# A hand-ordered prologue on one Trainium2 core: four loads, four value projections and two half units in another order

## The chip, the cores and the metric

The kernel runs on one NeuronCore of a Trainium2 chip. The metric is the device time of one execution in microseconds (us), and the time before is the median of three runs: 222.35 us (222.42, 222.35 and 222.23).

## The reference, cut to what matters

There are 2048 tokens of width 512, and `x` is used by both branches. `D` is 512, `F` is 1792.

```python
xn = layernorm(x)                                # no scale, no shift, eps 1e-5
q, k, v = split(xn @ wqkv)                       # 32 heads of 16
phi(t) = concat(softmax(t @ w_phi), softmax(-t @ w_phi))
kv = sum_s phi(k)[s]^T v[s] ;  z = sum_s phi(k)[s]
o = (phi(q) @ kv) / (phi(q) @ z + 1e-6)
out = x + o @ wo + ((xn @ w_gate) * (xn @ w_up)) @ w_down
```

## The kernel before, in words

The tokens are 16 tiles of 128 (`NT`), in four groups of four. Everything TensorE needs of a tile is its normalized and transposed form `xnT`, four chunks of 128 features by 128 tokens. Once that exists, a tile feeds three kinds of work:

- **v projection** (`vproj`, before.py's line 332, matmuls on L252): four matmuls 128x512 that accumulate in one PSUM bank, which is then copied to `vt` (L339).
- **a unit** (`unit`, L281): for one block of 128 hidden features and a whole group of tokens, four matmuls of the gate weights `wg` (name `g`), four of the up weights `wu` (name `u`), both on L288. ScalarE copies the gate to SBUF (`g_sb`, L294), VectorE multiplies (`hT`, L297). A half unit does two of the four tiles, with matmuls 128x256.
- k and q features, the attention and the output (`fin`), all later.

For the first group the normalization is done by hand, tile by tile: VectorE's statistics (L161, then an aggregate on L367, L382 or L393), ScalarE's square root (`std`, L371), VectorE's reciprocal (L375) and the application (`xn`, L177). TensorE transposes the four chunks into one PSUM bank (`tp`, L219), and ScalarE copies them to `xnT` in two halves (L223). The later groups take another path (`ln_block` and transposing DMAs), and the change doesn't touch it.

The order of the work is written out by hand: a manual schedule holds TensorE, VectorE, ScalarE, GpSimd and the SyncE queue to the order of the program text. All loads are issued by SyncE in that order too, on one queue (L74 to L100): x tiles 0 and 1, `wv` in two halves, x tiles 2 and 3, the first two blocks of `wg` and then of `wu`, `wphi`, and so on.

[...]

Before the first tile is ready, nine matmuls of constants (`warm_up(9)`, L324) keep TensorE at work; a tenth stands behind tile 0's transposes. Then TensorE's order is: transposes of tile 0, the warm-up, the first half of v of tile 0, transposes of tile 1, the rest of v of tile 0, v of tile 1, gate of half unit 0, transposes of tile 2, its up, gate of half unit 1, transposes of tile 3, its up, v of tiles 2 and 3. Then come the second halves of the two units (`for f in range(2)`, tiles 2 and 3), full units, the fold of the k weights (L243), and so on to the end without a further wait of note.

Of the kernel before, what the change touches and what calls it, by code (L numbers as in the profile page):

```python
# [8 lines left out]
BF16 = mybir.dt.bfloat16  # L9
F32 = mybir.dt.float32  # L10
# [11 lines left out]
def kernel(  # L22
# [51 lines left out]
    def dma_x(lo, hi):  # L74
        nc.sync.dma_start(out=xall[:, lo:hi, :], in_=x_view(lo, hi))  # L75
# [4 lines left out]
    def dma_gu(lo, hi):  # L80
        dma_cols(nc.sync, wg, B_w_gate, lo * P, hi * P)
        dma_cols(nc.sync, wu, B_w_up, lo * P, hi * P)
# [3 lines left out]
    for lo in (0, 2):  # L86
        nc.sync.dma_start(out=wv[:, lo:lo + 2, :],  # L87
                          in_=A_wqkv[lo * P:(lo + 2) * P, 2 * D:3 * D].rearrange("(c p) f -> p c f", p=P))
    dma_x(2, 3)
    dma_x(3, 4)  # L90
    dma_gu(0, 2)
    nc.sync.dma_start(out=wphi[:], in_=A_w_phi.rearrange("(c h) d f -> (h d) c f", c=DC))
    dma_gu(2, 4)
    nc.sync.dma_start(out=wT2[:, 1, :, :], in_=A_wqkv[:, D:2 * D], transpose=True)
# [12 lines left out]
    def table(func, i):  # L107
        nc.scalar.activation(out=first[:, i:i + 1], in_=ones[:, 0:1], func=func, scale=1.0)
# [45 lines left out]
    def bank(name, dt=F32, n=TT):  # L154
        return ps_s.tile([P, n], dt, name=name, tag="s")
# [3 lines left out]
    def ln_sums(n):  # L159
        stats = lnpool.tile([P, nc.vector.BN_STATS_DIM], F32, name="stats")  # L160
        nc.vector.bn_stats(out=stats[:], in_=xall[:, n, :])  # L161
        return stats
# [18 lines left out]
    def mv_tile():  # L181
        return lnpool.tile([P, GT, nc.vector.BN_AGGR_DIM], F32, name="mv", bufs=GT)
# [30 lines left out]
        for i in range(GT):  # L213
            chores.append(lambda i=i: apply(i))

    def lt(n, parts=1, later=False):
        tp = bank("tp", BF16).rearrange("p (c t) -> p c t", c=DC)
        for c in range(DC):
            nc.tensor.transpose(out=tp[:, c, :], in_=xns[n][:, c * P:(c + 1) * P], identity=ident[:])  # L219

        def copies():
            for c in range(0, DC, DC // parts):
                nc.scalar.copy(out=xnT[:, c:c + DC // parts, n * P:(n + 1) * P], in_=tp[:, c:c + DC // parts, :])  # L223

        if later:
            return copies
        copies()

    bd = consts.tile([P, DC, 8, DH], BF16)

# [19 lines left out]
    def proj(ps, n, w, js=range(DC)):  # L250
        for j in js:
            nc.tensor.matmul(ps, lhsT=xnT[:, j, n * P:(n + 1) * P], rhs=w[:, j, :],  # L252
                             start=(j == 0), stop=(j == DC - 1))
# [24 lines left out]
    hTs = {}  # L278
    units = [(T, f) for T in range(NGRP) for f in range(FC)]

    def unit(T, f, lo=0, hi=TT, amid=None):  # L281
        if T not in hTs:
            hTs[T] = hpool.tile([P, FC, TT], BF16, name="hT", tag="h")
        pss = []
        for w, name in ((wg, "g"), (wu, "u")):
            ps = bank(name)[:, 0:hi - lo]
            for c in range(DC):
                nc.tensor.matmul(ps, lhsT=w[:, c, f * P:(f + 1) * P], rhs=xnT[:, c, T * TT + lo:T * TT + hi],  # L288
                                 start=(c == 0), stop=(c == DC - 1))
            pss.append(ps)  # L290
            if amid is not None and name == "g":
                copies = amid()
        g_sb = gpool.tile([P, TT], BF16, name="g_sb")
        nc.scalar.copy(out=g_sb[:, 0:hi - lo], in_=pss[0])  # L294
        if amid is not None:
            copies()
        nc.vector.tensor_tensor(out=hTs[T][:, f, lo:hi], in0=pss[1], in1=g_sb[:, 0:hi - lo], op=ALU.mult)  # L297

    def ffn(k):
        for _ in range(k):  # L300
# [18 lines left out]

    warm = bank("warm")  # L320

    def warm_up(k):
        for _ in range(k):
            nc.tensor.matmul(warm, lhsT=ones[:, 0:P], rhs=ones, start=True, stop=True)  # L324

    warm_up(9)

    with tc.tile_pool(name="ps_k", bufs=1, space=PSUM) as ps_k:
        kvps = [ps_k.tile([P, 4, 4, E1], F32, name=f"kv{b}") for b in range(2)]
        phiks = {}  # L330

        def vproj(n, copy=nc.scalar.copy, amid=None, later=False):
            ps = bank("pv")
            proj(ps, n, wv, range(2))
            if amid is not None:
                amid()
            proj(ps, n, wv, range(2, DC))
            def evict():
                copy(out=vts[n % NV][:, :, :, 0:DH], in_=ps.rearrange("p (a b c) -> p a b c", a=8, b=4))  # L339
            if later:  # L340
                return evict
            evict()

        def kproj(n, pf=None):
            phiks[n] = features(n, W1k, "k", pf)

        def vkproj(n):
            pv, pk = bank("pv"), bank("k")
            for j in range(DC):
                proj(pv, n, wv, (j,))  # L350
                proj(pk, n, W1k, (j,))
            nc.scalar.copy(out=vts[n % NV][:, :, :, 0:DH], in_=pv.rearrange("p (a b c) -> p a b c", a=8, b=4))  # L352
            kproj(n, pk)

        def kv(n):
            vt, phik = vts[n % NV], phiks[n]
            for gr in range(NG):
                nc.tensor.matmul(kvps[gr // 4][:, gr % 4, :, :].rearrange("p a b -> p (a b)"),  # L358
                                 lhsT=phik[:, gr, :], rhs=vt[:, gr, :, :].rearrange("p a b -> p (a b)"),
                                 start=(n == 0 and gr % 4 == 0), stop=(n == NT - 1 and gr % 4 == 3))  # L360

        mvs = [mv_tile() for n in range(GT)]
        stds = {}

        def first_stats(n):
            stats = ln_sums(n)
            nc.vector.bn_aggr(out=mvs[n][:, 0, :], in_=stats[:])  # L367

        def first_std(n):
            stds[n] = lnpool.tile([P, 1], F32, name="std", bufs=GT)  # L370
            nc.scalar.activation(out=stds[n][:], in_=mvs[n][:, 0, 1:2], func=AF.Sqrt, bias=epst[:], scale=1.0)  # L371

        def first_apply(n):
            rstd = lnpool.tile([P, 1], F32, name="rs1", bufs=GT)
            nc.vector.reciprocal(out=rstd[:], in_=stds[n][:])  # L375
            ln_apply(n, mvs[n][:, 0, 0:1], rstd[:])

        first_stats(0)
        first_std(0)
        stats1 = ln_sums(1)  # L380
        first_apply(0)
        nc.vector.bn_aggr(out=mvs[1][:, 0, :], in_=stats1[:])  # L382
        first_std(1)
        first_apply(1)
        first_stats(2)
        stats3 = ln_sums(3)
        lt(0, parts=2)
        warm_up(1)
        copy_v = vproj(0, amid=lambda: lt(1, parts=2), later=True)
        first_std(2)  # L390
        first_apply(2)
        copy_v()
        nc.vector.bn_aggr(out=mvs[3][:, 0, :], in_=stats3[:])  # L393
        first_std(3)
        first_apply(3)
        make_bd()
        nc.gpsimd.tensor_tensor(out=M4[:], in0=BO[:, 0:4, :], in1=BO[:, 4:8, :], op=ALU.add)
        vproj(1)
        unit(0, 0, 0, 2 * P, amid=lambda: lt(2, parts=2, later=True))
        unit(0, 1, 0, 2 * P, amid=lambda: lt(3, parts=2, later=True))  # L400
        vproj(2, copy=nc.vector.tensor_copy)
        vproj(3, copy=nc.vector.tensor_copy)
        table(AF.Exp, 1)
        for f in range(2):
            unit(0, f, 2 * P, TT)
        del units[0:2]
        ffn(1)
        for j0 in (0, 2):
            fold(1, W1k, j0, (nc.scalar.copy, nc.vector.tensor_copy))
        ffn(1)  # L410
        ln_block(4)
        ffn(1)
        chore(2)
        kproj(0)
        ffn(1)
        chore(2)
        ffn(1)
        chore()
        kproj(1)
        ffn(1)  # L420
        chore()
        ffn(1)
        kproj(2)
        chore()
        ffn(1)
        kv(0)
        chore()
        ffn(1)
        kproj(3)
        chore()  # L430
        ffn(1)
        kv(1)
        nc.sync.dma_start(out=wT2[:, 0, :, :], in_=A_wqkv[:, 0:D], transpose=True)
        for n in range(GT, NT):
            if n in (4, 8):
                ln_block(n + 4)
            vkproj(n)
            chore(1 if n % GT < 2 else 0)
            ffn(1)
            kv(n - 2)  # L440
            chore((1, 2, 2, 2)[n % GT])
            if n >= 8 and n % 2 == 0:
                qproj((n - 8) // 2)
            if n == 6:
                fold(0, W1q, 0)
            ffn(1)
            if n == 6:
                fold(0, W1q, 2)
        ffn(1)
        kv(NT - 2)  # L450
        ffn(1)
        kv(NT - 1)
        for b in range(2):
            nc.vector.tensor_tensor(out=KV[:, 4 * b:4 * b + 4, :, :], in0=kvps[b][:],
                                    in1=_bcast_ap(M4[:], [M4[:].ap[0], [0, 4], [E1, 4], [1, E1]]), op=ALU.mult)
        qproj(4)
        ffn(1)
# [64 lines left out]
```

## Time and profile before

| what | value |
|---|---|
| median of three runs | 222.35 us |
| the profiled execution's own time | 222.45 us |
| its span, first to last instruction | 220.7 us |
| TensorE (PE) busy | 215.6 us, 98% of the span |
| VectorE (DVE), ScalarE (ACT), GpSimd (POOL) busy | 138.7, 89.5, 68.8 us |
| last transposes of the first group (tile 3) start | 10.25 us |
| second halves of the two units start on TensorE | 12.64 us |
| first fold starts | 16.21 us |

Times are counted from the start of the span. A line of the timeline has the start, the length, the engine, the line of the program, the operation, what it writes and reads, and how many instructions were merged; in brackets stands how long the engine had been idle, and what released it. PEld is the loading of a stationary operand, which can run beside a matmul. Matmul lengths in the profile reach past the start of the next one, so TensorE's pace is read from starts, not from lengths.

### The profile page before, as it was taken

The numbers are of one execution on the slowest core, as the hardware profiler recorded it, in microseconds if no ns is written. First come the engines' busy times: TensorE is split into PE (matmuls) and PEld (weight loads), VectorE is DVE, ScalarE is ACT, GpSimd is POOL, SyncE is SP. The second block draws the span as 40 slices with busy tenths as digits, with TensorE's granted clock in tenths as the row PEclk, the third lists the DMA queues.
The fourth block names the chain that finished last, engine by engine and source line by source line (L and its number), as shares of the span: only waits on it lengthen the run. The fifth ranks groups of instructions, "written<-read, shape, count | busy, mean of one in ns | idle before, by whom it ended". The sixth has DMA issues, their size and how long they took to land.

```text
span 220.7 us, 3490 instructions
## 1 busy us (share of the span) xinstructions
PE 215.6 (98%) x1284; PEld 104.8 (47%) x1308; DVE 138.7 (63%) x241; ACT 89.5 (41%) x170; POOL 68.8 (31%) x54
## 2 busy tenths in 40 slices
PE   8999999999999999999999999999999999999994
PEld 2554444445444444444544444444444444454443
DVE  4657985785569685757589964197645745454321
ACT  3755575449764875545353221231322323100000
POOL 3000455545335653637333643033033033000000
PEclk9999999999999999999999999999999999999999
DMA  5999983503200324020206645214431431422401
GB/s 182 237 310 386 367 217 69 97 0 48 31 18 12 57 43 81 9 42 1 49 1 96 119 97 109 62 24 95 95 74 24 95 71 28 91 52 71 71 27 48
DMA packets 47249, 19.91 MB, mean 90 GB/s; under 512 B 37504, under 2 KB 46976, under 8 KB 47104
## 3 DMA queue, kind: packets, MB, share of 16 engines
q1 hardware_dynamic: 47232, 19.69, 38.2%
q8 instruction: 10, 0.16, 0.3%
q14 instruction: 7, 0.06, 0.1%
HBM read 8.67 MB, written 2.10 MB: 49 GB/s over the span
## 4 chain that ended last, share of the span: by engine, by line
PE 94%; DMA 2%; SPq 1%; issue 1%; ACT 0%; DVE 0%
PE u L288 22%; PE fin L310 22%; PE g L288 21%; PE fin L313 6%; PE k L252 6%; PE q L252 6%; PE pv L252 5%; DMA wu<-in_B_w_up_dram 2%; PE ab L465 2%; PE kv L358 2%; SPq L75 1%; PE pq L243 1%; SPq L87 0%; SPq L78 0%; ACT g_sb L294 0%
## 5 line engine op out<-in xcount | busy, mean ns | idle before, releaser
L288 PE MATMUL u<-xnT,wu 128*128 128x512 bf16 (+1 forms) x229 | 57.7, 372 | 0.4
L288 PE MATMUL g<-xnT,wg 128*128 128x512 bf16 (+1 forms) x222 | 56.7, 372 | 0.4
L297 DVE TENSOR_TENSOR hT<-u,g_sb 128x512 bf16<-128x512 f32 (+1 forms) x58 | 37.3, 649 | 26.3 <-PE u L288 16.9
L265 DVE TENSOR_REDUCE sums<-e 128x64 f32<-128x1024 f32 x32 | 38.9, 1216 | 21.8 <-ACT e L262 21.8
L294 ACT CAST g_sb<-g 128x512 bf16<-128x512 f32 (+1 forms) x58 | 33.4, 576 | 45.9 <-PE g L288 45.7
L310 PE MATMUL fin<-wd,hT 128*128 128x512 bf16 (+2 forms) x234 | 50.9, 366 | 0.3
L269 POOL TENSOR_TENSOR phiq<-e,rs 128x1024 bf16<-128x1024 f32 x16 | 30.9, 1932 | 60.8 <-DVE rs L267 53.6
L269 POOL TENSOR_TENSOR phik<-e,rs 128x1024 bf16<-128x1024 f32 x16 | 30.9, 1932 | 55.5 <-DVE rs L267 44.0
L288 PEld LDWEIGHTS <-wu 128*128 128x128 bf16 x232 | 22.6, 98 | 25.8 <-DMA wu<-in_B_w_up_dram 0.2
L310 PEld LDWEIGHTS <-hT 128*128 128x128 bf16 x238 | 22.4, 98 | 24.7
L288 PEld LDWEIGHTS <-wg 128*128 128x128 bf16 x232 | 21.9, 98 | 23.4 <-DMA wg<-in_B_w_gate_dram 0.2
L252 PEld LDWEIGHTS <-xnT 128*128 128x128 bf16 x192 | 17.4, 98 | 18.7 <-ACT xnT L223 1.3
L316 DVE TENSOR_TENSOR o_sb<-fin,xall 128x512 bf16<-128x512 f32 (+2 forms) x17 | 11.2, 657 | 22.3 <-PE fin L313 22.2
L252 PE MATMUL pv<-wv,xnT 128*128 128x512 bf16 x62 | 22.1, 386 | 0.1
L252 PE MATMUL k<-W1k,xnT 128*128 128x512 bf16 x63 | 21.9, 379 | 0.1
L261 ACT ACTIVATE e<-q 128x512 f32<-128x512 f32 x16 | 9.5, 596 | 25.4 <-PE q L252 20.0
L267 DVE RECIPROCAL rs<-sums 128x64 f32<-128x64 f32 x32 | 17.7, 553 | 3.1
L313 PE MATMUL fin<-wo,oT 128*128 128x512 bf16 (+2 forms) x68 | 16.6, 367 | 0.0
L252 PE MATMUL q<-W1q,xnT 128*128 128x512 bf16 x60 | 15.9, 378 | 0.1
L352 ACT CAST vt<-pv 128x512 bf16<-128x512 f32 x12 | 7.0, 587 | 17.4 <-PE pv L252 17.4
L161 DVE BATCH_NORM_STATS2 stats<-xall 128x6 f32<-128x512 bf16 x16 | 10.7, 667 | 1.4 <-DMA xall<-in_A_x_dram 1.4
L474 DVE TENSOR_TENSOR otok<-ab,rden 128x512 bf16<-128x512 f32 x16 | 11.1, 691 | 0.6
(51 smaller groups left out, 118.6 us busy)
## 6 DMA issues: line engine op xcount, KB each, us to landing
out_dram<-o_sb SPq DMA_DIRECT2D x15, 128.0 KB, 2.0
wd<-in_B_w_down_dram SPq DMA_DIRECT2D x1, 1792.0 KB, 15.9
wg<-in_B_w_gate_dram SPq DMA_DIRECT2D x2, 640.0 KB, 6.8
wu<-in_B_w_up_dram SPq DMA_DIRECT2D x2, 640.0 KB, 8.0
xall<-in_A_x_dram SPq DMA_DIRECT2D x1, 1024.0 KB, 11.9
xall<-in_A_x_dram SPq DMA_DIRECT2D x4, 128.0 KB, 2.7
wv<-in_A_wqkv_dram SPq DMA_DIRECT2D x2, 256.0 KB, 3.0
wg<-in_B_w_gate_dram SPq DMA_DIRECT2D x2, 256.0 KB, 4.8
```

The source lines that it names most:

```text
L161: nc.vector.bn_stats(out=stats[:], in_=xall[:, n, :])
L252: nc.tensor.matmul(ps, lhsT=xnT[:, j, n * P:(n + 1) * P], rhs=w[:, j, :], start=(j == 0), stop=(j == DC - 1))
L265: nc.vector.tensor_reduce(out=sums[:], in_=ev, axis=AX.X, op=ALU.add)
L267: nc.vector.reciprocal(out=rs[:].rearrange("p a b -> p (a b)"), in_=sums[:])
L269: nc.gpsimd.tensor_tensor(out=phi[:].rearrange("p g (x f) -> p (g x) f", f=DH), in0=ev, in1=rs[:].to_broadcast((P, 2 * H, DH)), op=ALU.mult)
L288: nc.tensor.matmul(ps, lhsT=w[:, c, f * P:(f + 1) * P], rhs=xnT[:, c, T * TT + lo:T * TT + hi], start=(c == 0), stop=(c == DC - 1))
L294: nc.scalar.copy(out=g_sb[:, 0:hi - lo], in_=pss[0])
L297: nc.vector.tensor_tensor(out=hTs[T][:, f, lo:hi], in0=pss[1], in1=g_sb[:, 0:hi - lo], op=ALU.mult)
L310: nc.tensor.matmul(ps, lhsT=hTs[T][:, f, t4 * P:(t4 + 1) * P], rhs=wd[:, f, lo:lo + w], start=(f == 0), stop=False)
L313: nc.tensor.matmul(ps, lhsT=oTs[n][:, c, :], rhs=wo[:, c, lo:lo + w], start=False, stop=(c == DC - 1))
L316: nc.vector.tensor_tensor(out=o_sb[:], in0=ps, in1=xall[:, n, lo:lo + w], op=ALU.add)
L474: nc.vector.tensor_tensor(out=o_tok[:].rearrange("p (b h d) -> p b h d", b=2, d=DH), in0=abv[:, :, :, 0:DH], in1=rden[:].to_broadcast((P, ...
```

## The change

The change touches only the stretch up to the second halves. It

- issues the gate load ahead of x tile 3 (the up load stays behind it);
- lets tile 0's transposes go to two banks, two chunks each, so that the first copy waits for two transposes and not for four;
- adds a warm-up matmul of 256 columns behind the nine;
- gives v of tiles 0 and 1 two banks of their own (those that later hold the `kv` sums);
- puts TensorE's work in this order: tile 0's transposes, warm-up, half of v of tile 0, tile 1's transposes, the rest of v of tile 0, v of tile 1, gate of half unit 0, tile 2's transposes, gate of half unit 1, v of tile 2, both ups, tile 3's transposes, v of tile 3;
- puts VectorE's and ScalarE's work in the order that fits: tile 3's statistics come behind tile 2's application, the copies of v of tile 1 and of both gates ahead of tile 3's copies, `bd` (L233) behind both products.

The loop over later tiles is as it was. The core of the diff:

```diff
     dma_x(2, 3)
+    dma_cols(nc.sync, wg, B_w_gate, 0, 2 * P)
     dma_x(3, 4)
-    dma_gu(0, 2)
+    dma_cols(nc.sync, wu, B_w_up, 0, 2 * P)
...
+    def lt(n, nbanks=1):
+        step = DC // nbanks
+        tps = []
+        for lo in range(0, DC, step):
+            tp = bank("tp", BF16).rearrange("p (c t) -> p c t", c=DC)
+            for c in range(lo, lo + step):
+                nc.tensor.transpose(out=tp[:, c, :], in_=xns[n][:, c * P:(c + 1) * P], identity=ident[:])
+            tps.append(tp)
+        for lo in range(0, DC, 2):
+            nc.scalar.copy(out=xnT[:, lo:lo + 2, n * P:(n + 1) * P], in_=tps[lo // step][:, lo:lo + 2, :])
...
+    def half(w, name, T, f, lo, hi):
+        ps = bank(name)[:, 0:hi - lo]
+        for c in range(DC):
+            nc.tensor.matmul(ps, lhsT=w[:, c, f * P:(f + 1) * P], rhs=xnT[:, c, T * TT + lo:T * TT + hi],
+                             start=(c == 0), stop=(c == DC - 1))
+        return ps
...
     warm_up(9)
+    warm_up(1, 2 * P)
...
+    with tc.tile_pool(name="ps_v", bufs=1, space=PSUM) as ps_v:
+        pv = [ps_v.tile([P, D], F32, name=f"pv{n}") for n in range(2)]
+        first_std(0, ln_sums(0))
+        stats = ln_sums(1)
+        first_apply(0)
+        first_std(1, stats)
+        first_apply(1)
+        lt(0, nbanks=2)
+        warm_up(1)
+        proj(pv[0][:], 0, wv, range(2))
+        lt(1)
+        proj(pv[0][:], 0, wv, range(2, DC))
+        proj(pv[1][:], 1, wv)
+        first_std(2, ln_sums(2))
+        first_apply(2)
+        vcopy(0, pv[0])
+        g = [half(wg, "g", 0, 0, 0, 2 * P)]
+        lt(2)
+        g.append(half(wg, "g", 0, 1, 0, 2 * P))
+        pv2 = bank("pv")
+        proj(pv2, 2, wv)
+        stats = ln_sums(3)
+        g_sb = [gate_copy(g[0], 2 * P)]
+        first_std(3, stats)
+        first_apply(3)
+        g_sb.append(gate_copy(g[1], 2 * P))
+        vcopy(1, pv[1])
+        u0 = half(wu, "u", 0, 0, 0, 2 * P)
+        hidden(0, 0, u0, g_sb[0], 0, 2 * P)
+        vcopy(2, pv2, nc.vector.tensor_copy)
+        u1 = half(wu, "u", 0, 1, 0, 2 * P)
+        hidden(0, 1, u1, g_sb[1], 0, 2 * P)
+        lt(3)
+        pv3 = bank("pv")
+        proj(pv3, 3, wv)
+        make_bd()
+        vcopy(3, pv3, nc.vector.tensor_copy)
+        table(AF.Exp, 1)
...
-        first_stats(0)
-        first_std(0)
-        stats1 = ln_sums(1)
-        first_apply(0)
-        nc.vector.bn_aggr(out=mvs[1][:, 0, :], in_=stats1[:])
-        first_std(1)
-        first_apply(1)
-        first_stats(2)
-        stats3 = ln_sums(3)
-        lt(0, parts=2)
-        warm_up(1)
-        copy_v = vproj(0, amid=lambda: lt(1, parts=2), later=True)
-        first_std(2)
-        first_apply(2)
-        copy_v()
-        nc.vector.bn_aggr(out=mvs[3][:, 0, :], in_=stats3[:])
-        first_std(3)
-        first_apply(3)
-        make_bd()
-        nc.gpsimd.tensor_tensor(out=M4[:], in0=BO[:, 0:4, :], in1=BO[:, 4:8, :], op=ALU.add)
-        vproj(1)
-        unit(0, 0, 0, 2 * P, amid=lambda: lt(2, parts=2, later=True))
-        unit(0, 1, 0, 2 * P, amid=lambda: lt(3, parts=2, later=True))
-        vproj(2, copy=nc.vector.tensor_copy)
-        vproj(3, copy=nc.vector.tensor_copy)
-        table(AF.Exp, 1)
```

`first_std` now holds the aggregate too; `vcopy`, `gate_copy` and `hidden` are the copies and the product that `vproj` and `unit` held before.

More of the change, by code (lines that the diff above doesn't have):

```diff
@@ L214, in ln_block @@
             chores.append(lambda i=i: apply(i))
[L216 to L227, printed above, removed]
+    def lt(n, nbanks=1):
[8 more added lines that the diff above has]
+            nc.scalar.copy(out=xnT[:, lo:lo + 2, n * P:(n + 1) * P], in_=tps[lo // step][:, lo:lo + 2, :])
     bd = consts.tile([P, DC, 8, DH], BF16)
@@ L279, with gate_copy, hidden, unit @@
     units = [(T, f) for T in range(NGRP) for f in range(FC)]
-    def unit(T, f, lo=0, hi=TT, amid=None):
+    def half(w, name, T, f, lo, hi):
[4 more added lines that the diff above has]
+        return ps
+    def gate_copy(ps, n):
+        g_sb = gpool.tile([P, TT], BF16, name="g_sb")
+        nc.scalar.copy(out=g_sb[:, 0:n], in_=ps)
+        return g_sb
+    def hidden(T, f, ps, g_sb, lo, hi):
         if T not in hTs:
             hTs[T] = hpool.tile([P, FC, TT], BF16, name="hT", tag="h")
[L284 to L297, printed above, removed]
+        nc.vector.tensor_tensor(out=hTs[T][:, f, lo:hi], in0=ps, in1=g_sb[:, 0:hi - lo], op=ALU.mult)
+    def unit(T, f, lo=0, hi=TT):
+        pg = half(wg, "g", T, f, lo, hi)
+        pu = half(wu, "u", T, f, lo, hi)
+        hidden(T, f, pu, gate_copy(pg, hi - lo), lo, hi)
     def ffn(k):
@@ L320, with warm_up, vcopy @@
     warm = bank("warm")
-    def warm_up(k):
+    def warm_up(k, n=TT):
         for _ in range(k):
-            nc.tensor.matmul(warm, lhsT=ones[:, 0:P], rhs=ones, start=True, stop=True)
+            nc.tensor.matmul(warm[:, 0:n], lhsT=ones[:, 0:P], rhs=ones[:, 0:n], start=True, stop=True)
     warm_up(9)
+    warm_up(1, 2 * P)
+    def vcopy(n, ps, copy=nc.scalar.copy):
+        copy(out=vts[n % NV][:, :, :, 0:DH], in_=ps.rearrange("p (a b c) -> p a b c", a=8, b=4))
+    mvs = [mv_tile() for n in range(GT)]
@@ new lines, with first_std, first_apply @@
+    stds = {}
+    def first_std(n, stats):
+        nc.vector.bn_aggr(out=mvs[n][:, 0, :], in_=stats[:])
+        stds[n] = lnpool.tile([P, 1], F32, name="std", bufs=GT)
+        nc.scalar.activation(out=stds[n][:], in_=mvs[n][:, 0, 1:2], func=AF.Sqrt, bias=epst[:], scale=1.0)
+    def first_apply(n):
+        rstd = lnpool.tile([P, 1], F32, name="rs1", bufs=GT)
+        nc.vector.reciprocal(out=rstd[:], in_=stds[n][:])
+        ln_apply(n, mvs[n][:, 0, 0:1], rstd[:])
+    with tc.tile_pool(name="ps_v", bufs=1, space=PSUM) as ps_v:
[36 more added lines that the diff above has]
+        table(AF.Exp, 1)
+        nc.gpsimd.tensor_tensor(out=M4[:], in0=BO[:, 0:4, :], in1=BO[:, 4:8, :], op=ALU.add)
@@ L330 @@
         phiks = {}
[L332 to L342, printed above, removed]
         def kproj(n, pf=None):
@@ L351, in vkproj @@
                 proj(pk, n, W1k, (j,))
-            nc.scalar.copy(out=vts[n % NV][:, :, :, 0:DH], in_=pv.rearrange("p (a b c) -> p a b c", a=8, b=4))
+            vcopy(n, pv)
             kproj(n, pk)
@@ L360, in kv @@
                                  start=(n == 0 and gr % 4 == 0), stop=(n == NT - 1 and gr % 4 == 3))
[L362 to L376, printed above, removed]
-        first_stats(0)
-        first_std(0)
-        stats1 = ln_sums(1)
-        first_apply(0)
-        nc.vector.bn_aggr(out=mvs[1][:, 0, :], in_=stats1[:])
-        first_std(1)
-        first_apply(1)
-        first_stats(2)
-        stats3 = ln_sums(3)
-        lt(0, parts=2)
-        warm_up(1)
-        copy_v = vproj(0, amid=lambda: lt(1, parts=2), later=True)
-        first_std(2)
-        first_apply(2)
-        copy_v()
-        nc.vector.bn_aggr(out=mvs[3][:, 0, :], in_=stats3[:])
-        first_std(3)
-        first_apply(3)
-        make_bd()
-        nc.gpsimd.tensor_tensor(out=M4[:], in0=BO[:, 0:4, :], in1=BO[:, 4:8, :], op=ALU.add)
-        vproj(1)
-        unit(0, 0, 0, 2 * P, amid=lambda: lt(2, parts=2, later=True))
-        unit(0, 1, 0, 2 * P, amid=lambda: lt(3, parts=2, later=True))
-        vproj(2, copy=nc.vector.tensor_copy)
-        vproj(3, copy=nc.vector.tensor_copy)
-        table(AF.Exp, 1)
         for f in range(2):
```

## Prediction

> **What bounds the kernel now.** I read the page's chain first, then TensorE's timeline for the first 13 us, then the waits and single instructions in narrow windows.
>
> The chain's shares by engine:
>
> ```profile
> PE 94%; DMA 2%; SPq 1%; issue 1%; ACT 0%; DVE 0%
> ```
>
> TensorE is the bound, and behind 17 us its starts stand at 0.216 us for every 128x512 matmul; the waits of TensorE and its weight loads lie in the first 17 us. So whatever the change adds to or takes from TensorE's start into the second halves (12.64 us) reaches the end one for one: no later stall can take it up. The stretch itself, on TensorE's timeline:
>
> ```profile
> 0.82 4.00 PE L324 MATMUL warm<-const-bfloat16-1.0 128*128 128x512 bf16 x9 [0.82 <-PEq L506]
> 4.88 0.61 PE L219 MATMUL tp<-ident,xn 128*128 128x128 bf16 x4
> 5.28 0.63 PE L324 MATMUL warm<-const-bfloat16-1.0 128*128 128x512 bf16 x1
> 5.95 0.97 PE L252 MATMUL pv<-wv,xnT 128*128 128x512 bf16 x2
> 6.75 0.39 PE L219 MATMUL tp<-ident,xn 128*128 128x128 bf16 x4
> 6.98 1.66 PE L252 MATMUL pv<-wv,xnT 128*128 128x512 bf16 x6
> 8.48 0.60 PE L288 MATMUL g<-xnT,wg 128*128 128x256 bf16 x4
> 8.92 0.39 PE L219 MATMUL tp<-ident,xn 128*128 128x128 bf16 x4
> 9.37 0.61 PE L288 MATMUL u<-xnT,wu 128*128 128x256 bf16 x4
> ```
>
> Two things are to be seen. Up to 6.7 us TensorE runs at half rate: nine warm-ups start 0.43 apart, transposes 0.107; from 6.75 on transposes start 0.055 apart, the 128x512 matmuls 0.216, the 128x256 ones 0.109 (the column of the granted clock reads 1.00 throughout and does not show this). I call the change of rate the opening of the gate, at 6.72. And TensorE is dense but for four waits: 0.26 for tile 0's `xn` (4.62 to 4.87), 0.25 for tile 0's first copy (5.70 to 5.95), 0.20 for tile 1's first copy (7.41 to 7.605), 0.23 for the up weights (9.14 to 9.37). The last stands in the chain too:
>
> ```profile
> 4.15 5.17 DMA wu<-in_B_w_up_dram
> 9.37 0.61 PE u L288 x4
> ```
>
> The up load lands at 4.15 + 5.17 = 9.32. From 9.37 to 12.64 TensorE has no wait, because in this order tile 2's and tile 3's transposes are each followed by at least 0.44 us of other work before v of their tile.
>
> **How long a tile's copy takes.** From the weight loads and ScalarE around tile 1:
>
> ```profile
> 7.18 0.65 ACT L223 COPY xnT<-tp 128x256 bf16<-128x256 bf16 x2 [1.01 <-PE tp L219]
> 7.60 0.11 PEld L252 LDWEIGHTS <-xnT 128*128 128x128 bf16 x2 [0.52 <-ACT xnT L223]
> ```
>
> The last transpose starts at 6.92 and takes 0.22; ScalarE starts 0.04 later, at 7.18; the first half is copied in 0.37; TensorE takes it up 0.05 later. That is 0.68 from the last transpose's start, 0.63 from the end of its 0.055 slot. Where v of a tile stands right behind its transposes, TensorE waits 0.63; where other work stands between, that much less.
>
> **The change, part by part**, with the gate at 6.72 as recorded:
>
> - *Loads.* Eight DMAs stay eight. Up to the up load the queue carries the same bytes, so `wu` still lands at 9.32 and what follows it on SyncE is unmoved. `wg` (8.4) and x tile 3 (6.7) change places: x tile 3 at 8.35, `wg` at 8.35 less what x tile 3 took behind x tile 2 (6.72 - 6.08 = 0.64), so 7.71. Bounds for `wg`: 6.72, where x tile 3 lands now, and 8.35. TensorE asks for it at 8.36: no cost at either end.
> - *The warm-up of 256 columns*: 0.21 at half rate, 4.62 to 4.83, in the wait that ends at 4.87. Nothing.
> - *Tile 0 in two banks.* The first bank is complete two transposes earlier (0.214), at 5.27; ScalarE is free from 5.24, where tile 1's `std` ends. Copy at 5.31, v of tile 0 at 5.74 and not 5.95; the warm-up ends at 5.70 and is no hindrance. Part is lost again: the two matmuls and the first transposes now run wholly at half rate. They start 5.74, 6.14, 6.56; the gate opens among the transposes; the last one starts at 6.81 instead of 6.92. So 0.12 is left, tile 1's copies move with it, its wait stays about 0.2, and v of tile 1 runs 7.49 to 8.36 (now 7.605 to 8.48): **-0.12**.
> - *Gate, tile 2, gate.* 8.36 + 0.44 = 8.80; tile 2's `xn` is there at 8.55 (VectorE 0.12 earlier, since `std` follows tile 1's copies). Transposes to 9.02. No wait for `wu` here: **-0.23**.
> - *v of tile 2.* Only one half gate (0.44) lies between transposes and v: 0.63 - 0.44 = **+0.19**. Start 9.65, end 10.51. ScalarE is free for the copy: `std` of tile 2 and the copy of v end at 8.4.
> - *Both ups*: 10.51 to 11.39, `wu` long there. Tile 3's statistics start behind tile 2's application (8.5), not held by the load (8.35); its `std` waits on ScalarE behind a gate copy, to 10.0, and `xn` is there at 10.96. Tile 3's transposes at 11.39 don't wait.
> - *v of tile 3* stands right behind its transposes, with nothing between: **+0.63**. Start 12.24, end 13.11.
> - *The rest.* Behind tile 3's copies ScalarE loads the Exp table (1.28 + 0.20) and the next gate copy comes at 14.0, 0.3 after its gate; six banks rotate and the next wish for that one is the fold's (16.7). `bd` on VectorE ends at 13.0, wanted by the fold at 16.7. GpSimd's order is unchanged. Nothing.
>
> Sum: -0.12 - 0.23 + 0.19 + 0.63 = **+0.47**: second halves at 13.11 instead of 12.64.
>
> **The opening of the gate** is the one term that the row gives only once. Before is deaf to it: were the gate open from 4.87, its first gate half would still wait for `wg` (8.35) and its first up for `wu` (9.32), so 12.64 would stay. After has no load on its path before 9.65, so an early gate counts in full: first v at 5.63, v of tile 1 at 6.91, first gate 7.77, transposes 8.21, gate 8.43, v of tile 2 at 9.06, ups 9.92, transposes 10.80, v of tile 3 at 11.65, second halves at 12.54: **-0.10**. The ends are +0.47 (gate at 6.72) and -0.10 (open from the start). The record is nearer to the first; but there TensorE's row was broken twice before the gate opened (0.26 and 0.25), while after the change it is unbroken from 0.82 to 5.70 and broken by 0.03. An opening some half microsecond to a microsecond earlier is what I take, the middle: **+0.19**. I keep both ends.
>
> [...]
>
> The profiled execution took 222.45 (span 220.7 and 1.75 around it), 0.10 over the median. So 222.45 + 0.19 - 0.10 = 222.54, say 222.55.
>
> **Rivals.**
>
> - *The gate opens as recorded, or later* (up to 0.3 later adds up to 0.15): +0.47 to +0.6, 222.8 to 222.95. For it: the only row there is. 0.38, nearly all of it slower.
> - *The gate opens early*, by 5.2, whatever TensorE's breaks: -0.10 to +0.04, about 222.3. For it: before's three runs, within 0.19, cannot tell, since before is deaf to the gate. [...] 0.15.
> - *Faster: the up load.* Before waits for `wu` from 9.14, after asks for it only at 10.5. If in plain runs it lands later than in the profile, each 0.1 costs before 0.1 and after nothing. From 0.63 later (9.95) the +0.19 turns into -0.44. Against it: the profiled execution is slower than the median, not faster. 0.07, 221.9.
> - *The split does not do what it says*: ScalarE's margin is 0.07 (5.24 to 5.31); a `std` later by more delays the first copy and adds up to 0.1. Inside the range of the others.
>
> **The numbers.** The forecast, 0.40: 222.4 to 222.75. About 0.2%, 0.44 us, is what a measurement of this kernel can tell from no change. Faster 0.07 (the up load); slower 0.38 (the late gate, +0.47 and more); same 0.55 (forecast and early gate). The range from 222.2 to 223.0 takes in -0.10 and +0.6 with some 0.05 for the terms.
>
> **What would show it.** Wait of 0.6 us on TensorE ahead of v of tile 3, released by ScalarE, and 0.2 ahead of v of tile 2; none for `wu`; `wg` landing near 7.7 and x tile 3 near 8.4; first v at 5.7; the second halves at 12.5 to 13.1, by the place where the 0.43 steps turn to 0.216. Wrong it would be if v of tile 3 started without a wait, if `wg` landed behind 8.4, or if the end moved otherwise than TensorE at the second halves.

## The result, and the profile after

After takes 222.82 us in the median (222.41 to 223.09), before 222.37 (221.69 to 222.72), 22 runs each. The ratio is 1.0018, with a 95% interval from 1.0011 to 1.0025: slower by 0.40 us (0.24 to 0.56; the medians lie 0.45 apart), between the +0.19 that was forecast and the +0.47 of the sum with the clock's opening as in before's record. The change is clear of the noise, as this interval does not reach zero; the prediction had held 0.44 for the least that can be told from no change. The median lies inside the range from 222.2 to 223.0, but outside the 222.4 to 222.75 that the forecast itself was given; it falls where the rival of the late opening stands. The profiled execution of after took 222.58, its span 220.9.

The chain of after's page, its shares by engine:

```profile
PE 98%; ACT 0%; DVE 0%; issue 0%
```

The DMA share is gone from it: the up load, with 2% in before, holds nothing any more. TensorE's timeline of the same stretch as in the prediction, to the second halves (the last line):

```profile
4.99 0.61 PE L223 MATMUL tp<-ident,xn 128*128 128x128 bf16 x4
5.39 0.57 PE L327 MATMUL warm<-const-bfloat16-1.0 128*128 128x512 bf16 x1
5.85 0.60 PE L251 MATMUL pv<-wv,xnT 128*128 128x512 bf16 x2
6.29 0.39 PE L223 MATMUL tp<-ident,xn 128*128 128x128 bf16 x4
6.51 1.66 PE L251 MATMUL pv<-wv,xnT 128*128 128x512 bf16 x6
8.01 0.60 PE L283 MATMUL g<-xnT,wg 128*128 128x256 bf16 x4
8.45 0.39 PE L223 MATMUL tp<-ident,xn 128*128 128x128 bf16 x4
8.67 0.60 PE L283 MATMUL g<-xnT,wg 128*128 128x256 bf16 x4
9.30 1.04 PE L251 MATMUL pv<-wv,xnT 128*128 128x512 bf16 x4
10.18 1.04 PE L283 MATMUL u<-xnT,wu 128*128 128x256 bf16 x8
11.05 0.39 PE L223 MATMUL tp<-ident,xn 128*128 128x128 bf16 x4
11.90 1.04 PE L251 MATMUL pv<-wv,xnT 128*128 128x512 bf16 x4 [0.47 <-ACT xnT L226]
12.77 0.60 PE L283 MATMUL g<-xnT,wg 128*128 128x256 bf16 x4
```

Read it by starts. Eight ups of 0.109 run from 10.18 to 11.05, four transposes of 0.056 to 11.27, and v of tile 3 starts at 11.90: 0.63 in which TensorE issues nothing. (The bracket says 0.47, since it counts from the modelled end of the last transpose.) Ahead of v of tile 2, four gates from 8.67 end at 9.11, and v starts at 9.30: 0.19. In after's chain, in order of time, the long wait is a copy with nothing beside it:

```profile
11.21 0.24 PE tp L223 x4
11.45 0.02 issue
11.47 0.38 ACT xnT L226
11.85 0.05 issue
11.90 1.04 PE pv L251 x4
```

In all fourteen traces of this study the execution's time less the start of the second halves on TensorE lies between 209.78 and 209.87 us (before 222.45 - 12.64 = 209.81, after 222.58 - 12.77 = 209.81). So whatever happens ahead of that start reaches the end in full, and a trace's start can stand for its time.

### The profile page after: what moved, and what is told of

Read it like the earlier page. It is cut to its first block, busy times and chain, and to the rows that moved or that the text cites. A ratio compares the mean times of both kernels' runs of the same rounds, so it can differ in the third digit from the quotient of the medians.

```text
span 220.9 us, 3515 instructions
## 1 busy us (share of the span) xinstructions
PE 216.7 (98%) x1309; PEld 104.7 (47%) x1309; DVE 138.7 (63%) x241; ACT 89.4 (40%) x170; POOL 68.8 (31%) x54
## 3 DMA queue, kind: packets, MB, share of 16 engines
HBM read 8.67 MB, written 2.10 MB: 49 GB/s over the span
## 4 chain that ended last, share of the span: by engine, by line
PE 98%; ACT 0%; DVE 0%; issue 0%
PE g L283 22%; PE fin L313 22%; PE u L283 22%; PE pv L251 7%; PE fin L316 6%; PE k L251 6%; PE q L251 6%; PE warm L327 2%; PE ab L471 2%; PE kv L406 2%; PE pq L242 1%; PE tp L223 1%; ACT xnT L226 0%; DVE o_sb L319 0%
## 5 line engine op out<-in xcount | busy, mean ns | idle before, releaser
L283 PE MATMUL g<-xnT,wg 128*128 128x512 bf16 (+1 forms) x232 | 57.8, 372 | 0.0
L333 ACT CAST vt<-pv 128x512 bf16<-128x512 f32 x14 | 8.3, 590 | 17.4 <-PE pv L251 17.4
```

## The experiments

The times below are medians; a ratio is to the kernel before, run on the same chip beside it. Two kernels that were not run beside each other are best compared by their ratios.

**e1: tile 3's transposes between the ups.**

```diff
+        lt(3)
         u1 = half(wu, "u", 0, 1, 0, 2 * P)
         hidden(0, 1, u1, g_sb[1], 0, 2 * P)
-        lt(3)
```

> The changed kernel with one thing moved: tile 3's transposes stand between the two ups, not behind them. My theory: the wait of 0.63 us ahead of v of tile 3 is the copy chain with nothing beside it, so 0.44 of up work in it leaves 0.19; tile 3's xn (taken up at 10.68 in the trace of after) makes the transposes wait some 0.05. So 0.37 to 0.44 less than after: 222.4 to 222.45, within 0.1 of before. Rival (the wait is not paid for by the end, or another engine sets the pace): less than 0.15 off after.

Measured: 222.44 (11 runs), ratio 1.0008 (0.9998 to 1.0017), 0.38 under after by the medians and 0.22 by the ratios; the two intervals overlap. TensorE's timeline of e1:

```profile
10.23 0.60 PE L283 MATMUL u<-xnT,wu 128*128 128x256 bf16 x4
10.75 0.40 PE L223 MATMUL tp<-ident,xn 128*128 128x128 bf16 x4
10.98 0.60 PE L283 MATMUL u<-xnT,wu 128*128 128x256 bf16 x4
11.84 0.81 PE L251 MATMUL pv<-wv,xnT 128*128 128x512 bf16 x3 [0.26 <-ACT xnT L226]
```

The up from 10.98 to 11.42 now lies in the copy. (One of the four matmuls of v is missing from this trace, so 11.84 is its second; the first stood near 11.62.) That is 0.2 of wait instead of 0.63. The second halves start at 12.48 and not at 12.77, although in this trace the clock opened 0.19 later than in after's and x tile 0 landed 0.05 later. In the traces the wait is what the order made it; how much of it the time gives back (0.22 to 0.38) is less sure, since two of the eleven executions lie at 222.94 and 222.95.

**e2: tile 0's transposes in one bank again** (`lt(0)` for `lt(0, nbanks=2)`).

> The changed kernel with tile 0's transposes in one bank again. My theory: first v 0.21 later; with no load on the path before v of tile 2, this comes through with 0.12 (gate at 6.7, as the first matmuls then run longer at full rate) to 0.21 (gate early): 222.95 to 223.05. Rival (tile 0's copy hidden, as in before, behind the gate load): within 0.05 of after.

Measured: 222.67 (11 runs), ratio 1.0018 (1.0009 to 1.0026), the same as after's, and not the 222.95 to 223.05 that was expected. ScalarE's two copies of tile 0, first in e2, then in after:

```profile
5.66 0.65 ACT L226 COPY xnT<-tp 128x256 bf16<-128x256 bf16 x2 [0.28 <-PE tp L223]
```

```profile
5.42 0.65 ACT L226 COPY xnT<-tp 128x256 bf16<-128x256 bf16 x2
```

In the traces the two banks are worth 0.24 at the first v (5.85 against 6.09) and 0.25 at the second halves (12.77 against 13.02, the clock's opening, by the traces' own record of the clock, being 5.77 and 5.71; 0.03 of it is x tile 0, which landed later). In the medians and ratios nothing of it shows: a difference of 0.2 is as wide as the intervals. The low end of the times is the one hint: e2's eleven executions all lie at 222.61 or above, eight of after's 22 below. The gain is seen on the path and not confirmed in the times.

**e3: x tile 3 ahead of the gate columns.**

```diff
-    dma_cols(nc.sync, wg, B_w_gate, 0, 2 * P)
     dma_x(3, 4)
+    dma_cols(nc.sync, wg, B_w_gate, 0, 2 * P)
```

> The changed kernel with x tile 3 loaded ahead of the gate columns again, as in before. My theory: the gate columns land some 0.6 later (near 8.2 to 8.35 instead of 7.6 to 7.8), and the first gate half, wanted at 8.0 (gate of the clock early) to 8.36 (late), waits 0 to 0.35 for them, which nothing behind takes up: 222.85 to 223.15, and a wait for the gate load on TensorE. Rival (the load order is without effect, the first gate half is held by v of tile 1): within 0.05 of after's 222.82.

Measured: 222.78 (10 runs), ratio 1.0022 (1.0013 to 1.0032). The rival holds: the load order alone is not to be seen in after's time. In e3's trace the gate columns landed at 7.72 although they came second, the up columns at 8.72 and not 9.3, and the first gate half started at 7.95, right behind v of tile 1. The landings differ more from execution to execution than the order moves them: `wg` landed at 6.98 and 7.95 in two executions of after itself (e10, e11 below).

**e4: before, with the gate of half unit 1 ahead of the up of half unit 0** (the two units of L399 and L400 taken apart, their four halves and the transposes in the order g, tile 2, g, u, tile 3, u).

> The kernel before with one thing moved: the gate of half unit 1 ahead of the up of half unit 0, so that it lies in the wait for the up weights. My theory: that wait goes (0.23 with the gate at 6.7, 0.33 with an early one, since the first gate half then stands at 8.38 and the transposes end at 9.04), nothing else waits: 0.23 to 0.33 less than before, 222.05 to 222.15. Rival (the up load is not what holds before): no difference.

Measured: 222.09 (11 runs), ratio 0.9989 (0.9979 to 0.9999), 0.25 under before. TensorE's timeline of e4:

```profile
8.59 0.39 PE L219 MATMUL tp<-ident,xn 128*128 128x128 bf16 x4
8.81 0.60 PE L365 MATMUL g<-xnT,wg 128*128 128x256 bf16 x4
9.25 0.60 PE L365 MATMUL u<-xnT,wu 128*128 128x256 bf16 x4
```

Where before stood from 9.14 to 9.37, a gate half runs to 9.25, and the up follows without a wait. So this one swap is a gain, with an interval that ends just under 1; what after spoiled came with the rest of the order.

**e5: before, with tile 0 in two banks.**

```diff
-        lt(0, parts=2)
+        lt(0, parts=2, nbanks=2)
```

> The kernel before with tile 0's transposes in two banks, nothing else. My theory: v of tile 0 starts 0.21 earlier and all of it is given back at the waits for the gate (8.35) and up weights (9.32): within 0.05 of before. Rival (the start is on the path of before too): 0.12 to 0.21 less than before.

Measured: 222.32 (11 runs), ratio 0.9995 (0.9986 to 1.0004). TensorE's timeline of e5:

```profile
5.90 0.83 PE L256 MATMUL pv<-wv,xnT 128*128 128x512 bf16 x2
9.30 0.61 PE L292 MATMUL u<-xnT,wu 128*128 128x256 bf16 x4 [0.19 <-DMA wu<-in_B_w_up_dram]
```

x tile 0 landed 0.16 later than in before's trace (2.96 against 2.80) and the first v still starts a little earlier, but the up waits for its load as before, at 9.30. With that wait in the path, an earlier start is given back.

**e7 and e8: no warm-ups**, in after and in before. The matmuls left out are those of constants, whose results nobody reads.

> The changed kernel without any warm-up matmul (they compute nothing that is used). It tests what the half rate costs. My theory: TensorE's first work is at 4.9, the full rate comes 4.5 to 6 us behind it (9.3 to 10.9, as in the traces behind their first matmul), and after pays the half rate with little cover: second halves at 14.2 to 14.7, 224.0 to 224.5. Rival (the rate is bound to the time since the start of the program, not to TensorE's work): full rate by 6.7 again and at most 0.1 more than after.

> The kernel before without any warm-up matmul. My theory: full rate at 9.3 to 10.9 as for after without warm-ups; the waits for the loads take up the first part, up to about 7.5, so the second halves start at 13.5 to 14.2: 223.3 to 224.0, 0.5 to 0.7 below after without warm-ups. Rival (rate bound to the program's start): 222.4.

Measured: e7 224.42 (4 runs), ratio 1.0093 (1.0073 to 1.0113); e8 223.41 (4 runs), ratio 1.0055 (1.0033 to 1.0077), both where they were expected. So after loses 1.6, before 1.05. The distance between the two is 1.0 by the medians and 0.85 by the ratios, where 0.5 to 0.7 were expected and 0.4 is that of the kernels with warm-ups; with four executions each, spread over 1.2 and 1.4, this growth is not clear of the noise. TensorE's timeline of e7:

```profile
9.61 1.06 PE L283 MATMUL g<-xnT,wg 128*128 128x256 bf16 x4
10.46 0.59 PE L223 MATMUL tp<-ident,xn 128*128 128x128 bf16 x4
10.88 0.60 PE L283 MATMUL g<-xnT,wg 128*128 128x256 bf16 x4
```

The first four gates take 0.85 to the start of what follows and the transposes 0.42, at half rate; behind 10.88 gates start 0.109 apart. The opening lies at 10.87, 5.9 behind TensorE's first work at 4.93; in e8 near 8.7, 3.6 behind. With the warm-ups, the first of which starts at 0.82, it lay at 4.04 to 6.72; so in these two runs it went with TensorE's first work (4.93 and 5.06) and not with the start of the program. That before takes a late opening better than after, as it has loads to wait for anyway, fits the times but is not shown by them.

**e10 and e11: after, twice more**, for other openings.

> The changed kernel once more, for another pair of clock opening and start of the second halves. My theory: start = 12.5 (opening by 5) to 13.1 (opening at 6.7), 12.75 for 5.8, plus what x tile 0 lands later than 2.80; and the execution's time is that start plus 209.8. Rival (the start moves with the loads and not with the opening): a start that misses this by more than 0.15 while the opening is the same.

> The changed kernel a third time, as e10_after_again: start of the second halves 12.5 (opening by 5) to 13.1 (opening at 6.7) plus what x tile 0 lands later than 2.80, and time that start plus 209.8.

Measured: 222.56 and 222.61, with second halves at 12.69 and 12.78. Tile 0's transposes in e10:

```profile
5.00 0.40 PE L223 MATMUL tp<-ident,xn 128*128 128x128 bf16 x4
```

In both the clock opened before 5: these transposes stand at full rate (0.40 for the four against 0.61 in after), and the 256-column warm-up at 4.62 took 0.34 and 0.28 instead of 0.42. x tile 0 landed at 2.92 and 2.94. For an opening by 5 the expectation was 12.5 plus 0.12 to 0.14. e10 meets it within 0.07; in e11 the gate columns came at 7.95, and the first gate half waited 0.07 for them. That wait was not in the sum.

**e6, e12 and e9: a copy never without cover.** e6 keeps after's start and arranges the rest so that each copy has other work beside it. (`lt` takes `amid`, which it calls behind the first of its two copies.)

```diff
         warm_up(1)
         proj(pv[0][:], 0, wv, range(2))
-        lt(1)
+        stats = ln_sums(2)
+        lt(1, nbanks=2, amid=lambda: first_std(2, stats))
+        first_apply(2)
         proj(pv[0][:], 0, wv, range(2, DC))
         proj(pv[1][:], 1, wv)
-        first_std(2, ln_sums(2))
-        first_apply(2)
         vcopy(0, pv[0])
-        g = [half(wg, "g", 0, 0, 0, 2 * P)]
         lt(2)
-        g.append(half(wg, "g", 0, 1, 0, 2 * P))
+        g = [half(wg, "g", 0, f, 0, 2 * P) for f in range(2)]
         pv2 = bank("pv")
-        proj(pv2, 2, wv)
-        stats = ln_sums(3)
-        g_sb = [gate_copy(g[0], 2 * P)]
-        first_std(3, stats)
+        proj(pv2, 2, wv, range(3))
+        first_std(3, ln_sums(3))
         first_apply(3)
-        g_sb.append(gate_copy(g[1], 2 * P))
-        vcopy(1, pv[1])
+        g_sb = [gate_copy(g[f], 2 * P) for f in range(2)]
         u0 = half(wu, "u", 0, 0, 0, 2 * P)
         hidden(0, 0, u0, g_sb[0], 0, 2 * P)
+        lt(3)
+        vcopy(1, pv[1])
+        proj(pv2, 2, wv, range(3, DC))
         vcopy(2, pv2, nc.vector.tensor_copy)
         u1 = half(wu, "u", 0, 1, 0, 2 * P)
         hidden(0, 1, u1, g_sb[1], 0, 2 * P)
-        lt(3)
         pv3 = bank("pv")
         proj(pv3, 3, wv)
```

> The changed kernel with its start (loads, two banks for tile 0, own banks for v of tiles 0 and 1) and an order in which each copy has work beside it: tile 1's transposes in two banks as well and tile 2's std between its copies; v of tile 1, tile 2's transposes, both gates, three matmuls of v of tile 2, up 0, tile 3's transposes, the last matmul of v of tile 2, up 1, v of tile 3. My theory: the second halves start where the end is set (time less 209.82 in every trace so far), so it comes to 11.9 (clock early) to 12.3 (late), 221.7 to 222.1, 0.25 to 0.6 below before. Rival (tile 3's late load, or ScalarE's longer row, holds it instead): a wait ahead of tile 3's transposes, 222.2 and more.

Measured: 222.05 (12 runs, 221.72 to 223.09), ratio 0.9998 (0.9984 to 1.0011). The median is where it was expected, but five of twelve executions lie at 222.5 and above, and by the ratio the kernel is no faster than before. VectorE's row for tile 3 in e6's trace, and TensorE's next transposes:

```profile
8.36 0.69 DVE L162 BATCH_NORM_STATS2 stats<-xall 128x6 f32<-128x512 bf16 x1 [0.55 <-DMA xall<-in_A_x_dram]
```

```profile
9.67 0.60 PE L285 MATMUL u<-xnT,wu 128*128 128x256 bf16 x4
10.30 0.40 PE L223 MATMUL tp<-ident,xn 128*128 128x128 bf16 x4
```

The late load of x tile 3, harmless in after's order, now stands on the path: up 0 ends at 10.11, the transposes start at 10.30. That is 0.19, and this execution is still one of the fast ones (221.90).

> The kernel e6_covered once more, for a second look at what holds its slower executions. My theory: x tile 3's landing plus 1.97 (8.33 to 10.30 in the first trace) is the start of tile 3's transposes whenever that lies behind up 0's end, and the second halves come 1.75 behind it (10.30 to 12.05). Rival: the transposes start right behind up 0 and the time is made elsewhere.

Measured: 222.13. TensorE's timeline of e12:

```profile
10.09 0.60 PE L285 MATMUL u<-xnT,wu 128*128 128x256 bf16 x4
10.53 0.39 PE L223 MATMUL tp<-ident,xn 128*128 128x128 bf16 x4
```

There x tile 3 landed at 7.97, the transposes (10.53) stood right behind up 0, and the second halves came 1.74 later, at 12.27. This execution was later than e6's by its clock: opening at 6.67 instead of 5.80, tile 2's transposes at 8.35 instead of 7.92. None of the executions above 222.5 left a trace.

> The kernel e6_covered with x tile 3 loaded ahead of the gate columns, as in before. In e6's trace tile 3's statistics waited 0.55 for that load and TensorE 0.19 for tile 3's xn; its 12 runs lie apart, 221.72 to 223.09. My theory: x tile 3's landing sets those runs; loaded first (landing by 7.3 at the latest) it holds nothing, and the gate half, wanted at 8.15 to 8.5, waits at most 0.2 for columns that land at 7.7 to 8.35. So 221.8 to 222.1, 0.25 to 0.5 under before, and runs within 0.7. Rival (the spread has another cause: the clock, or the up load): the runs stay as far apart and the median within 0.1 of e6's 222.05.

Measured: 222.04 (11 runs, 221.56 to 222.33), ratio 0.9981 (0.9972 to 0.9990). TensorE's timeline of e9:

```profile
9.65 0.60 PE L285 MATMUL u<-xnT,wu 128*128 128x256 bf16 x4
10.09 0.39 PE L223 MATMUL tp<-ident,xn 128*128 128x128 bf16 x4
10.53 0.60 PE L285 MATMUL u<-xnT,wu 128*128 128x256 bf16 x4
10.96 1.03 PE L253 MATMUL pv<-wv,xnT 128*128 128x512 bf16 x4
11.83 0.60 PE L285 MATMUL g<-xnT,wg 128*128 128x256 bf16 x4
```

From 9.65 each start follows the one ahead of it at the full pace: 0.44 for four ups, 0.22 for tile 3's transposes and 0.22 for the last matmul of v of tile 2 (its slot at 10.31; its record is missing), 0.43 for up 1, 0.87 for v of tile 3. x tile 3 landed at 6.19 here. With x tile 3 first, the executions above 222.5 are gone, the median stays. What made them in e6 is not shown: they lie 0.6 to 1.2 above the traced execution, in which the late load cost 0.19, and the clock's opening is a rival (0.37 at tile 2's transposes between e6 and e12). e9 beats before by 0.19% and after by 0.37% (0.9981/1.0018), the latter not run beside it; the one edit between it and e6 is the load order that e3 had found without effect in after.

## Why the prediction was right, step by step

The number came out inside the range because the range took in both ends of the clock's opening; the account rests on the waits in the traces and not on the number.

- **TensorE is the bound and the start counts one for one.** Right: 209.78 to 209.87 between the second halves and the end, in fourteen traces.
- **The wait for the up load goes (-0.23).** Right; e4, with that part alone, gains 0.25.
- **The waits of +0.19 and +0.63.** Both measured to the hundredth, 0.19 and 0.63, released by ScalarE as forecast; e1 takes 0.44 of work into the second, and its wait falls to 0.2.
- **Tile 0 in two banks.** First copy at 5.42 and first v at 5.85, both 0.11 behind the 5.31 and 5.74 that were worked out, as x tile 0 is (2.91 against 2.80). That before would have hidden the gain agrees with e5; that after keeps it is seen in e2's trace and not in its times.
- **The loads.** In after's trace x tile 3 landed at 8.20 and `wg` at 7.79, against 8.35 and 7.71. But over the traces the same load moves by a microsecond, which the prediction left out. e3 shows no effect of the swap on after's time.
- **The opening of the clock.** This is the loosest term: +0.57 between its two ends, of which the middle was taken. The ends are about right: with the opening before 5, e10 starts its second halves at 12.69 (12.54 worked out, where the row's own steps come to 12.52, and x tile 0 0.12 late); the late end is only seen in e12, whose start is of the same kind: tile 2's transposes 0.43 later than e6's for an opening 0.87 later, 0.06 of it from x tile 0. But the term is no straight line. From an opening before 5 (e10) to one at 5.77 (after's trace) the start moves by 0.08, and then by about 0.4 to 6.7: ahead of the first v (5.75 in e10, 5.85 in after) TensorE waits for a copy in both, and only from there did the half rate count. With the middle opening after's trace is at 12.77, where 12.83 was forecast, and 12.93 with x tile 0's landing.
- **A term left out: x tile 0.** It landed at 2.80 in before's trace, the earliest of all, and at 2.85 to 2.98 in the other thirteen. Before is deaf to that too (it waits for `wu` at 9.32 in any case), after is not: +0.1.
- **A term that did not belong: -0.10.** The forecast's 222.55 takes off what before's profiled execution lies over before's median. As the time behind the second halves is the same in every trace, that excess lies ahead of 12.64, in a row that waits for `wu`; after's row does not wait for it (this is worked out; no run tests it alone). The worked-out start of 12.83 gives 12.83 + 209.81 = 222.64 as it stands, and 222.74 with x tile 0's 0.1, against the measured 222.82 (222.77 by the ratio).
- **What stays open.** That 222.74 comes so near is in part luck, since a middle opening was traced at 12.77 and not at 12.93. The median of 22 executions lies at 222.82 - 209.82 = 13.00, and the spread is 12.59 to 13.27. Late openings would explain it: an estimate from e6 and e12 (0.43 later for an opening 0.87 later) asks for one near 6.2 at 13.00. It isn't shown: all three traces of after have openings by 5.77, only three of the twelve traces with warm-ups open behind 6.2 (6.40 in e5, 6.67 in e12, 6.72 in before), and loads that land late (0.07 in e11) are mixed in. The times lie on both sides of the sum: twelve of the 22 executions lie above 222.74, the middle with x tile 0's landing.
- **The rivals.** The median lies where the late opening was priced (222.8 to 222.95), but no trace of after has that opening. The early one (about 222.3) came in e10 and e11, and they took 222.56 and 222.61: the worked-out 12.54, with x tile 0 later by 0.12 and 0.14 and in e11 the 0.07 for `wg`, comes to 222.47 and 222.56. The up load did not land later than in before's trace in any way that mattered: 8.2 to 9.4 in the traces with warm-ups. ScalarE's margin ahead of the first copy held: tile 1's `std` ends at 5.36, the copy starts at 5.42.
- **The guess that an unbroken row on TensorE brings the opening on** is not borne out: with the filling warm-up the openings lie from 4.04 to 6.67, without it from 5.30 to 6.72, and the 6.67 of e12 came behind an unbroken row. Beyond its later place without warm-ups (10.87 in e7, near 8.7 in e8) these traces do not show what sets it.

## What to carry to other kernels

Where an engine in strict order is the bound, count for every handover (transpose, copy, matmul) what stands between the two ends: 0.63 us of cover is needed here, and each edit that takes it away shows as a wait of just the rest: 0.19 behind 0.44 of work, 0.63 behind none. An earlier start was worth nothing where a load was waited for behind it (e5: first v at 5.90 and not 5.95, the up at 9.30 behind its load, ratio 0.9995), so a move is judged by the next wait that is late, not by itself. And an order can make a load matter that did not before: x tile 3's landing held nothing in after's order and cost 0.19 in e6's trace.

## What the runs showed of the hardware

The trace's own record of the full clock starts at 6.72 in before and at 5.77 in after, and is 215.04 us long in both; its start is the opening. Three traces (e8, e10, e11) have no such record, and their openings are read from the distance between starts. The opening fell elsewhere from execution to execution: from TensorE's first work to the opening it took 3.2 (e3) to 5.9 us (before, e7). The column of the granted clock does not show the half rate ahead of the opening (in before it reads 1.00 there); the distance between starts does, 0.427 against 0.216 for a 128x512 matmul. The landing of a load in the first microseconds is no constant either: the 256 KB of `wg`, issued at the same time, landed at 6.98, 7.79 and 7.95 in three executions of after.
